# Weight conversions let go earlier, and key features computed from the PSUM bank with the row maximum as bias, in a linear-attention and mixer kernel

## The chip, the cores and the metric

The kernel runs on one core of one Trainium2 chip. The metric is the time of one execution on the device in microseconds. The kernel before took 1147.82 us in the median of 3 runs (1147.16 to 1151.01).

## The reference

Linear attention over 8 batches, 8 heads, 576 tokens and 64 values a head, and behind it a mixer block (token mixing, then channel mixing), all in float32:

```
proj = x @ w_phi                                   # 64 -> 128 features
proj = proj - max(|proj|)  per token
phi  = concat(exp(proj), exp(-proj))               # for q and for k
kv, z = sum over tokens of k_phi * v, of k_phi
attn = (q_phi @ kv) / (q_phi @ z + 1e-6)
h = relu(x^T @ w_tok1) @ w_tok2                    # mixes the 576 tokens
u = x + h^T
out = u + relu(u @ w_ch1) @ w_ch2                  # 512 -> 1536 -> 512
```

## The kernel before

**Work and streams.** Heads are taken in 32 pairs: pair `i` holds two heads of batch `i // 4`. Five generators emit the work: `keys()`, `queries()`, `token_stream()`, `load_weights()` and `channel_stream()`. `weave` (line 628) calls them by a virtual clock with a share for each, and the framework's scheduler then fixes the order in which each engine takes its instructions. An engine takes them strictly in that order, so an instruction that waits holds all behind it.

**Keys.** A pair has five groups of keys, four of two 128-token units and a last one of a single unit. For a group TensorE makes the projection `ppk` (line 242 for the plain float32 pairs 0 to 7), VectorE reduces it to the largest absolute value `mxk` (line 252) and subtracts it into an SBUF tile `pmk` (line 254), ScalarE makes the exponentials `kp` of plus and minus `pmk` (line 298), and TensorE adds their products with the values into `pkv` (line 323). Pairs 0 to 3 use two banks of PSUM by turns for `ppk`; from pair 4 on there is a single one, under the tag `keys`. A bank is free for the next projection when all its readers are done: here the reduction and the subtraction.

**Queries.** They go the same way (`ppq`, `mxq`, `pmq`), then are transposed (`pt`, line 392), exponentiated (`qf`, line 399) and multiplied with `kv` into `pr` (line 430). For each pair and each of the two token segments VectorE normalises: an add of 1e-6 to the denominators `dn` (line 443), a reciprocal (444) and a product into `rows` (445).

**Conversions.** The weights arrive as float64 bits. `convert` (line 127) loads them with a DMA on the SyncE (SP) queue into one of four staging buffers, takes the absolute value on ScalarE (line 146), makes the float32 bits with four VectorE operations (lines 147 to 150), rounds them to the upper half on ScalarE (line 74) and leaves the lower half to a subtraction on GpSimd (line 77). There are 24 conversions of 128x512 for the channel mixing (tiles `bitsc`, weights `wc`), in the order: four of the first matrix, four of the second, and so three times. Channel mixing (`h` and `acc`, line 83) cannot begin its parts before they are converted.

**Gates.** `row_numerators` appends the denominators of pairs 0 to 3 to the list `gates` (line 440): entry 2i is pair i's first segment, 2i+1 its second. Conversion n waits for entry `GATES[n]`: in the emission by `turn_of` (line 156), and on the chip by a copy of one column on GpSimd (line 145), on which its absolute value waits. Conversions beyond the list wait for the last entry in the emission and get no copy:

```
GATES = [2, 3, 4, 5, 6, 6, 7, 7]
...
        g = GATES[min(n, len(GATES) - 1)]
        yield from until(lambda: len(gates) > g)
        return gates[g] if n < len(GATES) else None
```

Of the kernel before, what the change touches and what calls it, by code (L numbers as in the profile page):

```python
# [12 lines left out]
AF = mybir.ActivationFunctionType  # L13
ALU = mybir.AluOpType
# [4 lines left out]
B, H, S, D = 8, 8, 576, 64  # L19
NP = H // 2  # L20
# [5 lines left out]
PLAIN = 8  # L26
ROWS = 8
BURST = 8
GATES = [2, 3, 4, 5, 6, 6, 7, 7]
BORROWED = 18  # L30
STAGES = 4
LAST = 15
# [12 lines left out]
def mixer_kernel(ctx, tc, qk, vm, vt, w_phi, w1, w2, wc1, wc2d, out):  # L45
    nc = tc.nc

    cst = ctx.enter_context(tc.tile_pool(name="cst", bufs=1))
    wk = ctx.enter_context(tc.tile_pool(name="wk", bufs=2))
# [106 lines left out]
    def turn_of():  # L156
# [3 lines left out]
        ngated[0] += 1  # L160
# [56 lines left out]
    def less_max(ts, units, name, base=None, early=False):

        n, kind = len(units), name[0]
        if early and base == D:
            ps = ps_a.tile([P, 2, 2, F], F32, tag=f"a{nplain['k'] % 2}", name=f"pp{name}")
            nplain["k"] += 1
        elif early and base == 0 and (nplain["q"] % 2 == 0 or nplain["q"] >= BORROWED):
            ps = ps_h.tile([P, 2, 2, F], F32, tag="h", name=f"pp{name}")
            nplain["q"] += 1
        elif early and base == 0:
            ps = ps_w.tile([P, 2, 2, F], F32, tag="keys", name=f"pp{name}", bufs=1)
            nplain["q"] += 1  # L230
        elif kind == "k":
            ps = ps_w.tile([P, 2, 2, F], F32, tag="keys", name=f"pp{name}", bufs=1)
        else:
            ps = ps_w.tile([P, 2, 2, F], F32, name=f"pp{name}", **REST)
        for i, u in enumerate(units):
            t, c = (ts[1], 512) if u is None else (ts[u[0]], P * u[1])
            if base is None:
                nc.tensor.matmul(ps[:, i].rearrange("p two f -> p (two f)"), t[:, c:c + P],  # L238
                                 wp2.rearrange("p two f -> p (two f)"), start=True, stop=True)
            else:  # L240
                rows = slice(D, P) if name == "k0_0" else slice(0, P)
                nc.tensor.matmul(ps[:, i, 0], t[rows, c:c + P], wz[rows, base // D], start=True, stop=True)  # L242
# [12 lines left out]
        return pm

    nplain = {"k": 0, "q": 0}
    raws, pairs, kvs, loaded = {}, {}, {}, set()
# [2 lines left out]
    def load(i):  # L261

        raw = wk.tile([P, 2 * S], F32, tag="raw", name=f"raw{i}", bufs=1)
        lo, hi = (D if i <= PLAIN else 0), (D if i == B * NP else P)
        nc.sync.dma_start(raw[lo:hi], qk[i, lo:hi])
        raws[i] = raw

    def load_plain(i):

        out = []  # L270
        for k, (c, n) in enumerate(((0, 512), (512, 640))):
            t = wk.tile([P, n], F32, tag=f"{'kq'[i % 2]}{k}", name=f"pair{i}{k}", bufs=1)
            nc.sync.dma_start(t[D:], qk[i, D:, c:c + n])
            out.append(t)
        for k, (c, n) in enumerate(((0, 512), (512, 640))):
            nc.sync.dma_start(out[k][:D], qk[i + 1, :D, c:c + n])
        pairs[i] = out

    def keys():
        groups = [[(0, 0), (0, 1)], [(0, 2), (0, 3)], [(1, 0), (1, 1)], [(1, 2), (1, 3)], [None]]  # L280
        todo = None
        for i in range(B * NP):
            yield from until(lambda: i < 2 or i - 2 in asked)
            if i < PLAIN:
                load_plain(i)
            else:
                load(i)
            v_sb, queue = vtiles[i % 2], nc.sync if i else nc.scalar
            queue.dma_start(v_sb[:, 0:4].rearrange("p u j d -> p (u j) d")[:, :, :D], vm[i])
            for j in range(2):  # L290
                queue.dma_start(v_sb[j * D:(j + 1) * D, 4, j, :D], vt[i, j])
            plain = D if i < PLAIN else None
            ts = pairs[i] if i < PLAIN else stack(raws[i], D, f"k{i}")
            for g, us in enumerate(groups):
                pm = less_max(ts, us, f"k{i}_{g}", plain, i < NP)
                kp = wk.tile([P, 2, 2, F], F32, tag="kp", name=f"kp{i}_{g}")
                for sg in range(2):
                    nc.scalar.activation(kp[:, :len(us), sg], pm[:, :len(us)], AF.Exp, scale=1.0 - 2.0 * sg)  # L298
                yield 0.22
                if todo:  # L300
                    add_kv(*todo)
                    yield 0.82
                todo = (i, g, us, kp, v_sb)
        add_kv(*todo)
        yield 0.82
# [322 lines left out]
    def weave(streams):  # L628
# [3 lines left out]
        while streams:  # L632
# [58 lines left out]
```

## Time and profile before

| | |
|---|---|
| median of 3 runs | 1147.82 us |
| profiled execution, its own time | 1147.9 us |
| its span, first to last instruction | 1146.1 us |
| TensorE (PE) busy | 1117.9 us, 98% |
| VectorE (DVE) busy | 796.0 us, 69% |
| GpSimd (POOL) busy | 521.3 us, 45% |
| ScalarE (ACT) busy | 486.3 us, 42% |
| granted TensorE clock, mean | 0.995 |

The first three are one time seen three ways: what a run is timed at, what the profiled one took, and what its instructions span. The shares are means over a kernel whose stages differ, so a stage has to be looked at by itself. The granted clock is a share of full speed; it takes two levels, 1.0 (2.4 GHz) and 0.5 (1.2 GHz), and a figure between is a mean over a stretch.

### The profile page before, as it was taken

What the parts mean: (1) busy time and instruction counts of PE and PEld (TensorE: products, weight loads), DVE (VectorE), ACT (ScalarE), POOL (GpSimd) and SP (SyncE); (2) the same over time, 40 slices, a digit from 0 to 9 for tenths busy, and PEclk for the clock granted to TensorE, in tenths of its full rate; (3) what the DMA queues carried; (4) which work ended last, traced back from release to release, by engine and by line L of the source; (5) the groups of instructions that cost most, each with busy time, mean ns of one, the idle gap of its engine ahead of it and who ended that gap; (6) DMA issues with size and microseconds to landing.
All of it is one profiled execution on the core that took longest, in us unless ns stands there. A gap on an engine that the chain in (4) does not pass through costs nothing.

```text
span 1146.1 us, 24296 instructions
## 1 busy us (share of the span) xinstructions
PE 1117.9 (98%) x9280; PEld 1098.4 (96%) x9280; DVE 796.0 (69%) x1751; ACT 486.3 (42%) x1397; POOL 521.3 (45%) x671
## 2 busy tenths in 40 slices
PE   8998899999999999999999999999999999999998
PEld 7997799989999999999999999999999999999998
DVE  7779873478687797887787685775777878663111
ACT  4666552344444544444544343443454454331110
POOL 2234433265455565565555462653655656430000
PEclk9999899999999999999999999999999999999999
DMA  7534511111011111111111110111111110000000
GB/s 205 141 93 149 194 30 40 32 36 46 4 48 41 42 32 49 33 29 34 40 32 50 32 50 2 50 33 28 32 42 32 51 32 12 19 1 19 20 19 19
DMA packets 66164, 54.39 MB, mean 47 GB/s; under 512 B 44992, under 2 KB 56768, under 8 KB 66048
## 3 DMA queue, kind: packets, MB, share of 16 engines
q1 hardware_dynamic: 64528, 52.41, 15.7%
q8 instruction: 74, 1.21, 0.5%
q10 hardware_dynamic: 1520, 0.43, 0.2%
q14 instruction: 42, 0.34, 0.1%
HBM read 43.38 MB, written 9.44 MB: 46 GB/s over the span
## 4 chain that ended last, share of the span: by engine, by line
PE 84%; DVE 8%; DMA 2%; ACT 2%; POOL 2%; issue 1%; SPq 0%; DVEq 0%; POOLq 0%; ACTq 0%
PE h L83 25%; PE acc L83 25%; PE pkv L323 9%; PE pn L83 6%; PE ph L83 3%; PE pa L83 3%; PE pt L392 3%; PE pr L430 2%; PE ppk L238 2%; PE ppq L238 2%; DMA raw<-in_w 1%; DVE qh L76 1%; PE px L504 1%; PE ppq L242 1%; DVE bitsc L149 1%
## 5 line engine op out<-in xcount | busy, mean ns | idle before, releaser
L83 PE MATMUL acc<-gh,wc 128*128 128x256 f32 x1728 | 343.1, 283 | 0.0
L83 PEld LDWEIGHTS acc<-gh,wc 128*128 128x128 f32 x1728 | 275.3, 188 | 0.1
L83 PE MATMUL h<-uh,wc_h 128*128 128x256 f32 x864 | 245.5, 284 | 1.5 <-DVE gl L571 1.5
L83 PE MATMUL h<-uh,wc_l 128*128 128x256 f32 x864 | 245.0, 284 | 0.0
L83 PE MATMUL h<-ul,wc_h 128*128 128x256 f32 x864 | 243.5, 282 | 0.0
L83 PE MATMUL acc<-gl,wc 128*128 128x256 f32 x864 | 242.0, 282 | 0.0
L298 ACT ACTIVATE kp<-pmk 128x256 f32<-128x256 f32 (+1 forms) x320 | 109.3, 389 | 162.2 <-POOL pmk L254 141.4
L83 PEld LDWEIGHTS h<-uh,wc_h 128*128 128x128 f32 x864 | 162.6, 188 | 2.2 <-issue 1.3
L323 PE MATMUL pkv<-v,kp 128*128 128x65 f32 (+2 forms) x1152 | 160.7, 271 | 2.9 <-ACT kp L298 2.1
L83 PEld LDWEIGHTS h<-ul,wc_h 128*128 128x128 f32 x864 | 162.8, 188 | 0.1
L83 PEld LDWEIGHTS acc<-gl,wc 128*128 128x128 f32 x864 | 162.6, 188 | 0.0
L83 PEld LDWEIGHTS h<-uh,wc_l 128*128 128x128 f32 x864 | 162.5, 188 | 0.1
L323 PEld LDWEIGHTS pkv<-v,kp 128*128 128x128 f32 x1152 | 149.6, 193 | 4.6 <-ACT kp L298 3.0
L571 DVE SCALAR_TENSOR_TENSOR gl<-h,gh 128x512 fp32r<-128x512 f32 x108 | 73.8, 683 | 107.6 <-ACT gh L570 104.2
L77 POOL TENSOR_TENSOR ql<-qf,qh 128x320 fp32r<-128x320 f32 (+1 forms) x96 | 88.0, 916 | 116.3 <-DVE qh L76 103.5
L399 ACT ACTIVATE qf<-pt 128x320 f32<-128x320 f32 (+1 forms) x256 | 91.7, 411 | 95.7 <-PE pt L392 79.1
L570 ACT ACTIVATE gh<-h 128x512 fp32r<-128x512 f32 x108 | 64.9, 601 | 124.2 <-PE h L83 123.0
L76 DVE CAST qh<-qf 128x320 fp32r<-128x320 f32 (+1 forms) x192 | 90.2, 483 | 37.3 <-ACT qf L399 32.2
L83 PE MATMUL pn<-qh,kv 128*128 128x320 f32 (+1 forms) x384 | 99.7, 298 | 0.2 <-DVE qh L76 0.2
L551 POOL TENSOR_TENSOR ul<-xt,uh 128x64 fp32r<-128x64 f32 (+3 forms) x120 | 60.0, 525 | 82.6 <-ACT uh L550 81.9
L479 DVE RECIPROCAL den<-den 128x320 f32<-128x320 f32 (+1 forms) x48 | 93.5, 1949 | 0.9
L213 POOL TENSOR_TENSOR stk<-raw,stk 64x512 fp32r<-64x512 f32 (+1 forms) x48 | 68.9, 1436 | 47.2 <-DVE stk L212 38.7
(122 smaller groups left out, 2274.8 us busy)
## 6 DMA issues: line engine op xcount, KB each, us to landing
raw<-in_qk SPq DMA_DIRECT2D x23, 576.0 KB, 3.8
rawc<-in_wc SPq DMA_DIRECT2D x24, 512.0 KB, 4.2
v<-in_vm SPq DMA_DIRECT2D x31, 256.0 KB, 3.4
out_x<-xt SPq DMA_DIRECT2D x12, 256.0 KB, 2.1
out_x<-xt SPq DMA_DIRECT2D x16, 192.0 KB, 2.0
pair<-in_qk SPq DMA_DIRECT2D x16, 160.0 KB, 4.1
pair<-in_qk SPq DMA_DIRECT2D x16, 128.0 KB, 3.7
raw<-in_w SPq DMA_DIRECT2D x8, 256.0 KB, 5.0
```

Source lines behind the costliest of these rows:

```text
L76: eng_hi.tensor_copy(hi, raw)
L77: eng_lo.tensor_tensor(lo, raw, hi.bitcast(F32), op=ALU.subtract)
L83: nc.tensor.matmul(o, a, m, start=first and i == 0, stop=last and i == 2, skip_group_check=group_ok)
L213: nc.gpsimd.tensor_tensor(t[lo:lo + D], src, t[base:base + D].bitcast(F32), op=ALU.subtract)
L238: nc.tensor.matmul(ps[:, i].rearrange("p two f -> p (two f)"), t[:, c:c + P], wp2.rearrange("p two f -> p (two f)"), start=True, stop=True)
L298: nc.scalar.activation(kp[:, :len(us), sg], pm[:, :len(us)], AF.Exp, scale=1.0 - 2.0 * sg)
L323: nc.tensor.matmul(o, kp[:, n, sg], v, start=g == 0 and n == 0 and sg == 0, stop=u is None, skip_group_check=True)
L399: nc.scalar.activation(full, src, AF.Exp, scale=1.0 - 2.0 * sg)
L479: nc.vector.reciprocal(den, den)
L551: nc.gpsimd.tensor_tensor(l[:, d:d + n], t[:, c, o:o + n], h[:, d:d + n].bitcast(F32), op=ALU.subtract)
L570: nc.scalar.activation(gh, ph, AF.Relu)
L571: nc.vector.scalar_tensor_tensor(gl, ph, 0.0, gh.bitcast(F32), op0=ALU.max, op1=ALU.subtract)
```

## The change

It has two parts. First, the list `GATES` is longer and starts lower: nine conversions instead of six are let go by entry 6 (the first segment of pair 3, the fourth pair) or before, the first one by entry 1 instead of 2, and twelve instead of eight get a gate copy. Second, for the keys of pairs 2 to 7 the subtraction falls away. VectorE only negates the maximum into a column `nmx` (one buffer for all groups), and ScalarE reads the projection from its bank, with the negated maximum as bias for the positive exponential and the maximum itself for the negative one. As the bias belongs to a unit, a group of two units takes four ACTIVATEs of 128 columns instead of two of 256. The bank is now released by the last of them.

```
--- before.py
+++ after.py
@@ -26,7 +26,7 @@
 PLAIN = 8
 ROWS = 8
 BURST = 8
-GATES = [2, 3, 4, 5, 6, 6, 7, 7]
+GATES = [1, 2, 2, 3, 4, 4, 5, 6, 6, 7, 7, 7]
 BORROWED = 18
 STAGES = 4
 LAST = 15
@@ -250,9 +250,13 @@
             pr, eng = ps[:, :n, 0], nc.vector
         mx = column(wk, 2, tag=f"mx{kind}", name=f"mx{name}")
         nc.vector.tensor_reduce(mx[:, :n], pr, axis=AX.X, op=ALU.max, apply_absolute_value=True)
+        if base == D and not name.startswith(("k0_", "k1_")):
+            nmx = column(wk, 2, tag="nmx", bufs=1, name=f"nmx{name}")
+            nc.vector.tensor_scalar(nmx[:, :n], mx[:, :n], -1.0, None, op0=ALU.mult)
+            return pr, (nmx, mx)
         pm = wk.tile([P, 2, F], F32, tag=f"pm{kind}", name=f"pm{name}", bufs=1 if kind == "t" else 2)
         eng.tensor_tensor(pm[:, :n], pr, mx[:, :n].unsqueeze(2).to_broadcast([P, n, F]), op=ALU.subtract)
-        return pm
+        return (pm, None) if kind == "k" else pm
 
     nplain = {"k": 0, "q": 0}
     raws, pairs, kvs, loaded = {}, {}, {}, set()
@@ -292,10 +296,15 @@
             plain = D if i < PLAIN else None
             ts = pairs[i] if i < PLAIN else stack(raws[i], D, f"k{i}")
             for g, us in enumerate(groups):
-                pm = less_max(ts, us, f"k{i}_{g}", plain, i < NP)
+                pm, mx = less_max(ts, us, f"k{i}_{g}", plain, i < NP)
                 kp = wk.tile([P, 2, 2, F], F32, tag="kp", name=f"kp{i}_{g}")
                 for sg in range(2):
-                    nc.scalar.activation(kp[:, :len(us), sg], pm[:, :len(us)], AF.Exp, scale=1.0 - 2.0 * sg)
+                    if mx is None:
+                        nc.scalar.activation(kp[:, :len(us), sg], pm[:, :len(us)], AF.Exp, scale=1.0 - 2.0 * sg)
+                        continue
+                    for u in range(len(us)):
+                        nc.scalar.activation(kp[:, u, sg], pm[:, u], AF.Exp, scale=1.0 - 2.0 * sg,
+                                             bias=mx[sg][:, u:u + 1])
                 yield 0.22
                 if todo:
                     add_kv(*todo)
```

The list of numbers moves instructions on every engine. In the rows below `bitsc_e_c` or `bitsc_k` is the tile of a conversion, and lines after 252 are higher by 4 or 9 in the changed file (`pmq` 258, denominators 452 to 454, `kp` 303 or 306).

VectorE, the first conversion. Before, it stands among the queries and keys behind the denominators of pair 1's first segment (`dn_0_549`):

```order
L443 TENSOR_SCALAR dn_0_549<-pr_0_506 128x4
L444 RECIPROCAL dn_0_549<-dn_0_549 128x4
L252 TENSOR_REDUCE mxq_00_635<-ppq_00_632 128x2
L445 TENSOR_TENSOR rows_0_361<-pr_0_506,dn_0_549 128x2x2x64
L443 TENSOR_SCALAR dn_0_549<-pr_0_506 64x2
L252 TENSOR_REDUCE mxq_01_701<-ppq_01_698 128x2
L254 TENSOR_TENSOR pmq_00_637<-ppq_00_632,mxq_00_635 128x256
L444 RECIPROCAL dn_0_549<-dn_0_549 64x2
L252 TENSOR_REDUCE mxk_1_723<-ppk_1_720 128x2
L147 TENSOR_SCALAR bitsc_0_0_558<-bitsc_0_0_558 128x512
```

Now it stands behind the denominators of pair 0's second segment (`dn_1_447`), ahead of pair 1's (`dn_0_564`):

```order
L452 TENSOR_SCALAR dn_1_447<-pr_1_404 128x4
L453 RECIPROCAL dn_1_447<-dn_1_447 128x4
L252 TENSOR_REDUCE mxt_658<-ppt_656 128x1
L454 TENSOR_TENSOR rows_0_361<-pr_1_404,dn_1_447 128x2x2x64
L252 TENSOR_REDUCE mxk_3_636<-ppk_3_633 128x2
L147 TENSOR_SCALAR bitsc_0_0_453<-bitsc_0_0_453 128x512
L148 TENSOR_SCALAR bitsc_0_0_453<-bitsc_0_0_453 128x512
L258 TENSOR_TENSOR pmt_660<-ppt_656,mxt_658 128x128
L149 SCALAR_TENSOR_TENSOR bitsc_0_0_453<-rawc_0_0_451,bitsc_0_0_453 128x512
L258 TENSOR_TENSOR pmq_11_621<-ppq_11_616,mxq_11_619 128x256
L150 SCALAR_TENSOR_TENSOR bitsc_0_0_453<-rawc_0_0_451,bitsc_0_0_453 128x512
L255 TENSOR_SCALAR nmxk_3_638<-mxk_3_636 128x2
L452 TENSOR_SCALAR dn_0_564<-pr_0_519 128x4
```

It moved up by one segment, and all its four operations now lie where the old order had keys and queries alone.

VectorE, the last key group of pair 5 (`ppk_4`). Before, its subtraction `pmk_4_1507` runs amid the conversions of the second third (`2_512`, `3_512`, and `4` of the second matrix):

```order
L252 TENSOR_REDUCE mxk_4_1505<-ppk_4_1503 128x1
L444 RECIPROCAL dn_0_1370<-dn_0_1370 64x2
L147 TENSOR_SCALAR bitsc_3_512_1335<-bitsc_3_512_1335 128x512
L148 TENSOR_SCALAR bitsc_2_512_1303<-bitsc_2_512_1303 128x512
L147 TENSOR_SCALAR bitsc_4_1384<-bitsc_4_1384 128x512
L254 TENSOR_TENSOR pmk_4_1507<-ppk_4_1503,mxk_4_1505 128x128
L445 TENSOR_TENSOR rows_0_1369<-pr_0_1259,dn_0_1370 64x128
L148 TENSOR_SCALAR bitsc_3_512_1335<-bitsc_3_512_1335 128x512
L149 SCALAR_TENSOR_TENSOR bitsc_2_512_1303<-rawc_2_512_1301,bitsc_2_512_1303 128x512
```

Now the negation `nmxk_4_1573` in its place stands amid those of the last third (`2_1024`, `3_1024`):

```order
L149 SCALAR_TENSOR_TENSOR bitsc_2_1024_1553<-rawc_2_1024_1551,bitsc_2_1024_1553 128x512
L148 TENSOR_SCALAR bitsc_3_1024_1597<-bitsc_3_1024_1597 128x512
L252 TENSOR_REDUCE mxq_01_1762<-ppq_01_1759 128x2
L252 TENSOR_REDUCE mxk_4_1571<-ppk_4_1569 128x1
L150 SCALAR_TENSOR_TENSOR bitsc_2_1024_1553<-rawc_2_1024_1551,bitsc_2_1024_1553 128x512
L149 SCALAR_TENSOR_TENSOR bitsc_3_1024_1597<-rawc_3_1024_1595,bitsc_3_1024_1597 128x512
L258 TENSOR_TENSOR pmq_01_1764<-ppq_01_1759,mxq_01_1762 128x256
L255 TENSOR_SCALAR nmxk_4_1573<-mxk_4_1571 128x1
L150 SCALAR_TENSOR_TENSOR bitsc_3_1024_1597<-rawc_3_1024_1595,bitsc_3_1024_1597 128x512
L252 TENSOR_REDUCE mxk_0_1651<-ppk_0_1648 128x2
L255 TENSOR_SCALAR nmxk_0_1653<-mxk_0_1651 128x2
```

Measured by conversions, the keys of pair 5 slid back: by that point ten conversions were finished before, and nineteen now.

ScalarE at the same place. Before, the group's exponentials come in one row (two ACTIVATEs, out of `pmk`), a row of pair 6 seven rows later:

```order
L146 ACTIVATE bitsc_4_1384<-rawc_4_1382 128x512
L146 ACTIVATE bitsc_5_1412<-rawc_5_1410 128x512
L298 ACTIVATE kp_4_1509<-pmk_4_1507 128x128 x2
L457 COPY xt_1_1449<-pf_0_1451 128x320
L399 ACTIVATE qf_110_1515<-pt_11_1512 128x256
L399 ACTIVATE qf_111_1517<-pt_11_1512 128x256
L74 CAST wc_h<-bitsc_2_512_1303 128x512
L332 COPY kv_5_1640<-pkv_1296 128x260
L74 CAST wc_h<-bitsc_3_512_1335 128x512
L298 ACTIVATE kp_0_1588<-pmk_0_1586 128x2x128 x2
```

Now they read the bank `ppk_4_1569` and stand between the roundings of the last third:

```order
L74 CAST wc_h<-bitsc_1_1024_1530 128x512
L466 COPY xt_1_1518<-pf_1_1766 128x256
L74 CAST wc_h<-bitsc_2_1024_1553 128x512
L306 ACTIVATE kp_4_1575<-ppk_4_1569,nmxk_4_1573 128x128
L306 ACTIVATE kp_4_1575<-ppk_4_1569,mxk_4_1571 128x128
L74 CAST wc_h<-bitsc_3_1024_1597 128x512
L341 COPY kv_5_1709<-pkv_1359 128x260
L306 ACTIVATE kp_0_1655<-ppk_0_1648,nmxk_0_1653 128x128 x2
L306 ACTIVATE kp_0_1655<-ppk_0_1648,mxk_0_1651 128x128 x2
```

The exponentials of pair 6's first group follow four rows behind them, and they are four ACTIVATEs.

## Rows read from the trace of the kernel before

**Rows 1.** The page: the span; busy time, share of the span and instructions of each engine; and the granted TensorE clock in tenths in 40 equal slices of the span.

```profile
span 1146.1 us, 24296 instructions
...
PE 1117.9 (98%) x9280; PEld 1098.4 (96%) x9280; DVE 796.0 (69%) x1751; ACT 486.3 (42%) x1397; POOL 521.3 (45%) x671
...
PEclk9999899999999999999999999999999999999999
```

**Rows 2.** Sums by stretch (us from the span's start): its length, then busy time and instructions of PE, of its weight loads, of DVE, ACT and POOL, then the granted clock, the DMA engines' busy share and GB/s.

```profile
35.00:78.40 43.40, 42.52 (x364) 40.75 (x362) 30.10 (x86) 25.02 (x70) 11.09 (x15) 1.00 0.47 129
78.40:133.30 54.90, 46.55 (x339) 43.04 (x338) 53.23 (x121) 33.84 (x80) 25.29 (x23) 0.91 0.47 149
...
146.00:240.00 94.00, 93.92 (x807) 92.69 (x807) 47.86 (x116) 35.69 (x99) 32.72 (x42) 1.00 0.10 31
```

**Rows 3.** Waits between 78.4 and 133.3 us: who waited for whom, us in total, how often, the longest.

```profile
ACT bitsc L146 <- DMA rawc<-in_wc: 4.6, 5, 1.4
...
PE ppk L242 <- DVE pmk L254: 2.6, 2, 2.4
...
PE ph L83 <- DVE xt L539: 1.7, 1, 1.7
PE pf L456 <- DVE rows L445: 1.6, 1, 1.6
...
PE ph L83 <- DVE al L530: 0.7, 1, 0.7
```

**Rows 4.** VectorE's instructions in order of time: start, duration, line, operation and tiles; in brackets the idle time before and what ended it. Three places of the same stretch.

```profile
78.45 0.16 DVE L443 TENSOR_SCALAR dn<-pr 128x4 f32<-128x4 f32 x1 [2.16 <-PE pr L430]
...
114.13 0.41 DVE L252 TENSOR_REDUCE mxq<-ppq 128x2 f32<-128x256 f32 x1
114.46 0.40 DVE L254 TENSOR_TENSOR pmk<-ppk,mxk 128x256 f32<-128x256 f32 x1
...
115.82 1.76 DVE L149 SCALAR_TENSOR_TENSOR bitsc<-rawc,bitsc 128x512 uint32<-128x512 uint32 x1
...
133.05 0.39 DVE L254 TENSOR_TENSOR pmk<-ppk,mxk 128x256 f32<-128x256 f32 x1
```

**Rows 5.** VectorE's instructions by line and form between 78.4 and 133.3 us: count, busy us in all, mean ns of one, and the engine's idle time before them.

```profile
L149 DVE SCALAR_TENSOR_TENSOR bitsc<-rawc,bitsc 128x512 uint32<-128x512 uint32 x14 | 13.0, 934 | 0.0
L150 DVE SCALAR_TENSOR_TENSOR bitsc<-rawc,bitsc 128x512 uint32<-128x512 uint32 x13 | 10.6, 825 | 0.0
L147 DVE TENSOR_SCALAR bitsc<-bitsc 128x512 f32<-128x512 f32 x14 | 8.7, 624 | 0.1
L148 DVE TENSOR_SCALAR bitsc<-bitsc 128x512 uint32<-128x512 uint32 x14 | 6.6, 476 | 0.0
L254 DVE TENSOR_TENSOR pmk<-ppk,mxk 128x256 f32<-128x256 f32 x9 | 3.7, 411 | 0.0
L252 DVE TENSOR_REDUCE mxk<-ppk 128x2 f32<-128x256 f32 x9 | 3.7, 410 | 0.1
...
L444 DVE RECIPROCAL dn<-dn 128x4 f32<-128x4 f32 x5 | 0.8, 169 | 0.0
...
L254 DVE TENSOR_TENSOR pmk<-ppk,mxk 128x128 f32<-128x128 f32 x2 | 0.6, 276 | 0.0
```

**Rows 6.** Sums by stretch as in rows 2, in slices of 2 us.

```profile
114.00:116.00 2.00, 1.08 (x5) 1.08 (x6) 2.00 (x6) 1.34 (x3) 2.00 (x2) 0.66 0.83 262
116.00:118.00 2.00, 1.85 (x9) 1.55 (x8) 2.00 (x3) 1.07 (x2) 1.03 (x1) 0.50 0.95 301
...
120.00:122.00 2.00, 1.14 (x7) 0.88 (x7) 2.00 (x5) 1.92 (x5) 1.23 (x1) 0.86 0.30 47
122.00:124.00 2.00, 2.00 (x10) 1.88 (x10) 2.00 (x6) 1.00 (x4) 0.04 (x1) 0.50 1.01 406
124.00:126.00 2.00, 2.00 (x11) 1.88 (x12) 2.00 (x6) 0.48 (x1) 0.00 (x0) 0.50 0.19 76
126.00:128.00 2.00, 2.00 (x10) 1.67 (x9) 1.84 (x5) 0.00 (x0) 0.00 (x0) 0.50 0.00 0
```

**Rows 7.** VectorE in order of time, the four operations of the fourth conversion, ahead of the stretch of rows 3 to 5.

```profile
72.45 0.42 DVE L147 TENSOR_SCALAR bitsc<-bitsc 128x512 f32<-128x512 f32 x1
72.90 0.43 DVE L148 TENSOR_SCALAR bitsc<-bitsc 128x512 uint32<-128x512 uint32 x1
73.36 0.69 DVE L149 SCALAR_TENSOR_TENSOR bitsc<-rawc,bitsc 128x512 uint32<-128x512 uint32 x1
74.08 0.70 DVE L150 SCALAR_TENSOR_TENSOR bitsc<-rawc,bitsc 128x512 uint32<-128x512 uint32 x1
```

**Rows 8.** ScalarE's exponentials by form between 78.4 and 133.3 us, as in rows 5; `pmk` lies in SBUF, `pt` in PSUM.

```profile
L298 ACT ACTIVATE kp<-pmk 128x256 f32<-128x256 f32 x16 | 5.8, 414 | 1.8 <-DVE pmk L254 1.7
...
L399 ACT ACTIVATE qf<-pt 128x256 f32<-128x256 f32 x10 | 3.3, 381 | 1.8 <-PE pr L430 1.3 <-PE pt L392 0.5
...
L298 ACT ACTIVATE kp<-pmk 128x128 f32<-128x128 f32 x4 | 1.0, 300 | 0.3 <-DVE pmk L254 0.3
```

**Rows 9.** GpSimd in order of time: two subtractions for lower halves in one row (x2), and a single one.

```profile
112.86 4.16 POOL L77 TENSOR_TENSOR wc_l<-bitsc,wc_h 128x512 fp32r<-128x512 f32 x2 [5.81 <-ACT wc_h L74]
118.21 1.28 POOL L77 TENSOR_TENSOR wc<-bitsc,wc 128x512 fp32r<-128x512 f32 x1 [1.18 <-ACT wc L74]
```

More of the change, by code (lines that the diff above doesn't have):

```diff
@@ L28 @@
 BURST = 8
-GATES = [2, 3, 4, 5, 6, 6, 7, 7]
+GATES = [1, 2, 2, 3, 4, 4, 5, 6, 6, 7, 7, 7]
 BORROWED = 18
@@ L252, in less_max @@
         nc.vector.tensor_reduce(mx[:, :n], pr, axis=AX.X, op=ALU.max, apply_absolute_value=True)
+        if base == D and not name.startswith(("k0_", "k1_")):
+            nmx = column(wk, 2, tag="nmx", bufs=1, name=f"nmx{name}")
+            nc.vector.tensor_scalar(nmx[:, :n], mx[:, :n], -1.0, None, op0=ALU.mult)
+            return pr, (nmx, mx)
         pm = wk.tile([P, 2, F], F32, tag=f"pm{kind}", name=f"pm{name}", bufs=1 if kind == "t" else 2)
         eng.tensor_tensor(pm[:, :n], pr, mx[:, :n].unsqueeze(2).to_broadcast([P, n, F]), op=ALU.subtract)
-        return pm
+        return (pm, None) if kind == "k" else pm
     nplain = {"k": 0, "q": 0}
@@ L294, in keys @@
             for g, us in enumerate(groups):
-                pm = less_max(ts, us, f"k{i}_{g}", plain, i < NP)
+                pm, mx = less_max(ts, us, f"k{i}_{g}", plain, i < NP)
                 kp = wk.tile([P, 2, 2, F], F32, tag="kp", name=f"kp{i}_{g}")
                 for sg in range(2):
-                    nc.scalar.activation(kp[:, :len(us), sg], pm[:, :len(us)], AF.Exp, scale=1.0 - 2.0 * sg)
+                    if mx is None:
+                        nc.scalar.activation(kp[:, :len(us), sg], pm[:, :len(us)], AF.Exp, scale=1.0 - 2.0 * sg)
+                        continue
+                    for u in range(len(us)):
+                        nc.scalar.activation(kp[:, u, sg], pm[:, u], AF.Exp, scale=1.0 - 2.0 * sg,
+                                             bias=mx[sg][:, u:u + 1])
                 yield 0.22
```

## The prediction

> **What bounds the kernel.** I read the page first, then sums by stretch, then the waits inside the one bad stretch. TensorE (PE) is busy 1117.9 us of a span of 1146.1 [rows 1]; the profiled execution took 1147.9 us, 1.8 more than its span and 0.1 over the median of 1147.82. So time can only come out of the places where PE stands still or runs at half clock. The sums show one such place [rows 2]: from 146 to 240 us PE works 93.92 of 94.00 us with 807 matmul records (a float32 matmul makes two), or 0.1164 us per record, the pace at full clock. From 78.4 to 133.3 us it gets through only 339 records in 54.9 us. At full pace they need 339 x 0.1164 = 39.5 us, so 15.4 us are lost there, and VectorE (DVE) is busy 53.23 of the 54.9. Before it, from 35 to 78.4, PE loses 0.9 us and DVE is busy 30.10 of 43.40: DVE has 13.3 us free.
>
> The waits of the bad stretch agree [rows 3]: PE's waits end with DVE work (pmk 2.6, xt 1.7, rows 1.6, al 0.7). So DVE's list between two places sets this stretch: from the add on the denominators of pair 4's first segment, which DVE begins at 78.45 after waiting 2.16 us for PE, to the pmk of pair 6's fourth group at 133.05 [rows 4].
>
> **The change: what DVE no longer does.** For pairs 2 to 7 the subtraction pmk goes (24 of 128x256, 6 of 128x128); a negation of 2 numbers comes in its place. Large DVE operations start 0.33 us apart (114.13, 114.46) while their mean is 0.41 [rows 4, 5], so I price the large ones 0.08 under their means. The negation has no row. From below it is free; above, the reciprocal of 128x4 at 0.169 [rows 5]. I take 0.10, a small operation that overlaps as the large ones do. Whole kernel: 24 x (0.33 - 0.10) + 6 x (0.20 - 0.10) = 6.1 us less on DVE. That is not the gain: only DVE's list up to the place where PE waits counts.
>
> **What moves.** In the new order seven conversions instead of four stand before the denominators of pair 4's first segment. That is three times 2.24 us (0.42 + 0.43 + 0.69 + 0.70) [rows 7], 6.7 us, less 13 subtractions swapped for negations, 11 x 0.23 + 2 x 0.10 = 2.7. The 4.0 us go into the 13.3 us that DVE has free from 35 to 78.4 [rows 2]: price 0. Without that cover the bounds are -0.9 (PE's whole loss there disappears) and +1.0 (a quarter of the extra work shows).
>
> But keys slid back against conversions. Before, the sharpest place is pair 6's fourth group. Now a crowd of conversions stands ahead of pair 5's **last** group: DVE negates that maximum only after 19 conversions and three of the four operations of the twentieth, while before ten were done when the pmk of that group ran (the order above). PE needs the exponentials of that group for its next pkv, and pair 6's first projection needs the bank that those free. So the new stretch ends there. Counted in the two orders from the same denominators to the end:
> - before: 121 DVE instructions, 54.9 us; PE 339 records.
> - after: 106 DVE instructions; PE 262 records, 262 x 0.1164 = 30.5 us.
>
> DVE's time after, from the difference of the two lists: one conversion less, 0.93 + 0.82 + 0.62 + 0.47 - 4 x 0.08 = 2.5; nine large pmk, 3.0; two small, 0.4; four mxk, 1.3; one mxq and one pmq, 0.7; one denominator add and reciprocal, 0.2; against them one xt more, 0.3, and seven negations, 0.7. Net 7.0 less [rows 5], 47.9 us if DVE's idle 1.7 us (54.9 - 53.23) comes back, 46.2 if not. I take 47.0. PE's loss is then 47.0 - 30.5 = 16.5 against 15.4: **+1.1 us** (+0.3 to +2.0). DVE does less, but it must be done 77 records earlier. Behind that place four conversions are left over many records, and PE loses only what it does now (0.08 us from 146 to 240).
>
> **The clock.** In the bad stretch the granted clock falls to 0.50, the lower level of 1.2 GHz, from 116 to 118 and again from 122 to 128, both behind slices with PE busy for little over half (1.08 and 1.14 of 2.00) [rows 6]. From 122 to 128 PE is busy all 6 us at half clock, and DVE is busy for 5.84 of them: what PE loses is hidden under DVE. After the change DVE has little left at that point and PE a full queue, so the same half-clock stretch would be paid. Bounds: 0, and half of the 6 us, 3.0. I take 1.0, a third, since part of it will fall into the waiting itself. The Trainium skill, page TensorE: Matmul & The Clock Gate, section HAM oscillation, says that a burst of matmuls behind idle gaps starts throttled, and that each gap is paid again; by that rule this term would be the full 3.0. By that rule the second drop is no accident, and the trace agrees: it stands behind the slice with 1.14 of 2.00 busy.
>
> **Queues.** ScalarE takes each group of keys as four ACTIVATEs of 128 columns with a column as bias, in place of two of 256. The nearest rows are 0.30 for 128 columns from SBUF, 0.41 for 256, and 0.38 for 256 out of a bank [rows 8]; four at 0.22 to 0.30 are 0.9 to 1.2 us against 0.7 to 0.8. Seven groups in the stretch add 0.5 to 3.5 us to an engine that is idle for over a third of it (33.84 of 54.9) [rows 2]: price 0, unless a release waits for it (third rival). The Trainium skill, page ScalarE: Activation LUTs, section What ACT_TABLE_LOAD costs, speaks against the change here: it gives 93 ns more for each ACTIVATE with a pointer operand; by it an estimate is 0.4 us more per group, and the sum would stay, as ScalarE is still not full. No run here has shown such a bias yet. GpSimd gets four more gate copies in an engine busy 25.29 of 54.9: 0. On SP the conversions' loads now stand ahead of more pair loads, and behind a load that waits for its staging buffer the pair loads wait too; ScalarE's waits for such loads were 4.6 us in all [rows 3] under DVE's shadow, so 0, at most +1. The negated column has one buffer: DVE must wait for the two exponentials of the group before. In the order other DVE and ScalarE work lies between; 0, at most +1.
>
> **Sum:** 1147.9 + 1.1 + 1.0 = **1150.0 us**, 0.19% over the median: no change, leaning slow. Own range of this case: from the lower bounds of all terms, 1147.9 + 0.3 - 0.9 = 1147.3, to the upper ones of the stretch and the clock, 1147.9 + 2.0 + 3.0 = 1152.9.
>
> **Rivals.**
> - *Faster: less crowding* (0.28). A conversion costs DVE 2.84 us in the bad stretch and 2.24 just before it [rows 5, 7]; one L149 took 1.76 at 115.82 while two GpSimd subtractions took 4.16 instead of 2 x 1.28 [rows 4, 9]. If starting earlier spaces DVE's and GpSimd's halves apart, 13 conversions give back up to 13 x 0.6 = 7.8: 1147.9 + 1.1 - 7.8 = 1141.2; half of it 1145.1. It decides when the mean L149 of the stretch is under 0.75 (0.934 now). Against it: the conversions stand even closer.
> - *Slower: the clock after the burst* (0.23). Place: the first 6 to 7 us behind pair 5's last group. PE has fewer matmuls between DVE's releases than now and then a full queue at half clock. Price 3.0, and 1.7 more if the first drop is also paid (2 us at 0.50, and 0.66 for 2 us, which is 1.4 us at 0.50): 1147.9 + 1.1 + 4.7 = 1153.7. It decides as soon as PE is busy over 90% at 0.50 while DVE is idle. For it: rows 6; against it: the waits may end at another phase.
> - *Slower: the single bank* (0.07). From pair 4 on all key projections share one bank, which DVE freed with pmk and ScalarE now frees with its fourth exponential, some 0.6 us later (4 x 0.22 to 0.30 against one pmk of 0.33 to 0.41). Seven groups in the stretch: 7 x 0.6 = 4.2, at 1147.9 + 1.1 + 4.2 = 1153.2. It decides when that release, not the negation, comes last. For it: PE already waited 2.6 us for pmk [rows 3].
> - That the change does not do what it says is ruled out by the order: 30 pmk are gone, and the first conversion stands a segment earlier.
>
> **Numbers.** The forecast has 0.42. About 0.3% (3.4 us) is what a measurement of this kernel can tell from no change: under 1144.4 is faster, over 1151.3 slower. Of the first rival 0.23 lies under 1144.4 and 0.05 above (less than half the relief). Of the forecast 0.36 lies between and 0.06 over 1151.3, where the clock is paid in full. Of the clock rival 0.20 is slower and 0.03 between; the bank's 0.07 is slower. So faster 0.23, same 0.36 + 0.05 + 0.03 = 0.44, slower 0.06 + 0.20 + 0.07 = 0.33. The range leaves out the far end of the fast case and the tail of the slow ones, two in ten: 1142.0 to 1155.5.
>
> **What would show it.** Right: DVE full from about 78 to about 125; a long wait of PE that ends with kp (line 306) of pair 5's last group, near 124 to 127; a stretch of clock 0.50 behind it; from 150 on PE full again; DVE's total about 6 us lower and all conversions done ahead of pair 7's first key group. Wrong if PE makes its records in the bad stretch faster than one per 0.15 us (55 / 339 = 0.162 now, 47 / 262 = 0.179 forecast), if the mean L149 falls under 0.75, or if PE's waits name kp in pairs 4 and 5 one group after another (the single bank).

## The result, and the profile after

The changed kernel takes 1154.73 us (median of 5 runs, 1153.10 to 1155.16) against 1147.51 beside it: ratio 1.0052, 95% interval 1.0037 to 1.0066 (the two medians alone would give 1.0063). So it is slower, by a little more than the 0.3% that the prediction took as the least that can be told from no change. The profiled execution took 1153.33 us, 5.4 more than that of before, and so did its span (1151.5 against 1146.1).

The page of the changed kernel: span, busy time by engine, and the granted clock in 40 slices.

```profile
span 1151.5 us, 24387 instructions
PE 1119.5 (97%) x9280; PEld 1100.7 (96%) x9280; DVE 788.5 (68%) x1751; ACT 495.3 (43%) x1445; POOL 525.4 (46%) x675
PEclk9999799999999999999999999999999999999999
```

VectorE (DVE) does 7.5 us less (796.0 before), and TensorE (PE) still sets the time. So I count PE's matmul records by stretch, as for before. Sums by stretch of the kernel before (the columns are those of [rows 2]):

```profile
0.00:78.40 78.40, 74.08 (x588) 69.24 (x588) 56.18 (x166) 43.10 (x118) 19.25 (x37) 1.00 0.58 158
78.40:140.00 61.60, 52.96 (x392) 49.23 (x391) 59.77 (x135) 37.69 (x90) 29.27 (x26) 0.92 0.48 153
140.00:400.00 260.00, 255.66 (x2141) 251.23 (x2141) 175.16 (x393) 111.62 (x328) 125.25 (x159) 1.00 0.13 37
```

The same stretches of the changed kernel, and the two parts of the bad one:

```profile
0.00:78.40 78.40, 74.13 (x579) 68.51 (x580) 62.34 (x177) 51.01 (x145) 24.23 (x43) 1.00 0.67 176
78.40:140.00 61.60, 47.30 (x337) 44.18 (x337) 54.10 (x123) 34.93 (x88) 31.56 (x25) 0.86 0.45 139
140.00:400.00 260.00, 257.45 (x2165) 253.88 (x2164) 164.64 (x390) 113.67 (x341) 121.17 (x155) 1.00 0.12 35
...
78.70:128.93 50.23, 35.93 (x263) 33.54 (x263) 45.55 (x107) 29.74 (x76) 28.46 (x23) 0.89 0.44 132
...
128.93:140.00 11.07, 11.07 (x71) 10.41 (x72) 8.54 (x17) 5.13 (x13) 3.10 (x3) 0.73 0.48 161
```

At 0.1164 us per record: by 78.4 us PE is 9 records behind (1.0 us), from 78.4 to 140 another 55 (6.4 us), and from 140 to 400 it wins back 24 (2.8 us). That leaves 4.7 of the 5.4 us.

What PE waits for between 30 and 150 us in the changed kernel (us in total, times, longest):

```profile
PE pkv L332 <- ACT kp L306: 11.2, 4, 4.3
PE pa L83 <- POOL xl L77: 2.5, 2, 2.2
PE pf L465 <- DVE rows L454: 1.3, 1, 1.3
...
PE ppk L242 <- ACT kp L306: 0.2, 1, 0.2
```

The waits of [rows 3] (pmk, xt, rows, al) are gone but for the rows. In their place PE waits for exponentials of keys (`kp`), and for GpSimd. The two longest are those of pair 5's fourth and last groups. In order of time, PE's first matmuls behind them, in the changed kernel:

```profile
120.61 1.73 PE L332 MATMUL pkv<-v,kp 128*128 128x128 f32 x6 [4.28 <-ACT kp L306]
...
128.93 1.23 PE L332 MATMUL pkv<-v,kp 128*128 128x130 f32 x4 [3.70 <-ACT kp L306]
```

What VectorE did between the maximum of each of those groups (mxk) and its negation (nmxk):

```profile
115.23 0.41 DVE L252 TENSOR_REDUCE mxk<-ppk 128x2 f32<-128x256 f32 x1
115.56 0.27 DVE L252 TENSOR_REDUCE mxt<-ppt 128x1 f32<-128x128 f32 x1
117.16 0.78 DVE L147 TENSOR_SCALAR bitsc<-bitsc 128x512 f32<-128x512 f32 x1 [1.33 <-ACT bitsc L146]
117.86 1.78 DVE L150 SCALAR_TENSOR_TENSOR bitsc<-rawc,bitsc 128x512 uint32<-128x512 uint32 x1
119.56 0.41 DVE L252 TENSOR_REDUCE mxq<-ppq 128x2 f32<-128x256 f32 x1
119.90 0.15 DVE L255 TENSOR_SCALAR nmxk<-mxk 128x2 f32<-128x2 f32 x1
...
125.86 0.28 DVE L252 TENSOR_REDUCE mxk<-ppk 128x1 f32<-128x128 f32 x1
126.06 1.41 DVE L150 SCALAR_TENSOR_TENSOR bitsc<-rawc,bitsc 128x512 uint32<-128x512 uint32 x1
127.40 0.68 DVE L149 SCALAR_TENSOR_TENSOR bitsc<-rawc,bitsc 128x512 uint32<-128x512 uint32 x1
128.00 0.41 DVE L258 TENSOR_TENSOR pmq<-ppq,mxq 128x256 f32<-128x256 f32 x1
128.33 0.14 DVE L255 TENSOR_SCALAR nmxk<-mxk 128x1 f32<-128x1 f32 x1
```

Conversions stand between the maximum and the 0.15 us that PE needs. In the first case there is an idle 1.33 us as well, for ScalarE, which itself waited 2.1 us for GpSimd's subtractions (`wc`).

Behind the second wait the clock is at its lower level. Sums by 2 us of the changed kernel:

```profile
130.00:132.00 2.00, 2.00 (x10) 1.72 (x10) 0.86 (x3) 0.89 (x2) 1.25 (x1) 0.50 1.04 350
132.00:134.00 2.00, 2.00 (x12) 2.00 (x11) 0.61 (x3) 1.85 (x6) 0.03 (x1) 0.50 0.48 172
```

From 130 to 134 PE is full at 0.50 (1.2 GHz) while VectorE has 1.47 us of work in 4: the half clock that VectorE's list hid before [rows 6] is now paid.

### The profile page after: what moved, and what is told of

The parts are those of the page before. It is cut to its first block, busy times and chain, and to the rows that moved or that the text cites. A ratio compares the mean times of both kernels' runs of the same rounds, so it can differ in the third digit from the quotient of the medians.

```text
span 1151.5 us, 24387 instructions
## 1 busy us (share of the span) xinstructions
PE 1119.5 (97%) x9280; PEld 1100.7 (96%) x9280; DVE 788.5 (68%) x1751; ACT 495.3 (43%) x1445; POOL 525.4 (46%) x675
## 4 chain that ended last, share of the span: by engine, by line
PE 84%; DVE 9%; POOL 2%; issue 2%; ACT 2%; DMA 1%; SPq 0%; DVEq 0%; POOLq 0%; ACTq 0%
PE h L83 25%; PE acc L83 25%; PE pkv L332 9%; PE pn L83 6%; PE ph L83 3%; PE pa L83 3%; PE pt L401 3%; PE ppk L238 2%; PE ppq L238 2%; PE pr L439 2%; DVE qh L76 1%; PE px L513 1%; PE ppk L242 1%; PE ppq L242 1%; DVE bitsc L150 1%
## 5 line engine op out<-in xcount | busy, mean ns | idle before, releaser
L332 PE MATMUL pkv<-v,kp 128*128 128x65 f32 (+2 forms) x1152 | 164.7, 271 | 12.9 <-ACT kp L306 11.2
L303 ACT ACTIVATE kp<-pmk 128x256 f32<-128x256 f32 x260 | 88.8, 389 | 140.1 <-POOL pmk L258 134.6
```

Source lines behind the costliest of these rows:

```text
L332: nc.tensor.matmul(o, kp[:, n, sg], v, start=g == 0 and n == 0 and sg == 0, stop=u is None, skip_group_check=True)
```

## The experiments

All twelve change the changed kernel, or the kernel before, in one or two places. The theories: **A**, the crowd: VectorE's conversions stand too close together ahead of PE's needs. **B**, the key path: negation and four exponentials make every group slower. **C**, the earlier gates cost by themselves. **N**, it is VectorE's negation. **D**, conversions that come too late hold up the first channel block.

The table gives what each order has and what it took. "Ahead" counts the conversions that VectorE has finished, in its order, ahead of the subtraction or negation of pair 5's last key group and of pair 6's fourth (where ScalarE negates, of the maximum). The next columns are PE's records and mean granted clock from 78.4 to 140 us and its records from 140 to 400 us. The last ones are the median and the ratio to the kernel before, run beside it: its median was 1147.51 us beside the change, 1149.30 beside e1 to e4, 1148.19 beside e5 to e8 and 1149.24 beside e9 to e12, so kernels run beside different ones are best compared by the ratio. The records are those of the one profiled execution, which can lie 2 us or more from the median (e2 1147.51, e6 1147.53, e4 1147.29).

| kernel | ahead | 78.4–140 | 140–400 | us | ratio (95%) |
|---|---|---|---|---|---|
| before | 10 / 17 | 392, 0.92 | 2141 | 1147.51 | |
| the change | 19 / 22 | 337, 0.86 | 2165 | 1154.73 | 1.0052 (1.0037–1.0066) |
| e1 gates | 12 / 18 | 421, 0.94 | 2164 | 1142.08 | 0.9942 (0.9929–0.9955) |
| e2 keys | 15 / 19 | 382, 0.92 | 2164 | 1149.55 | 1.0008 (0.9997–1.0018) |
| e3 change, ScalarE negates | 17 / 22 | 420, 0.92 | 2165 | 1144.80 | 0.9969 (0.9957–0.9982) |
| e4 change, share 6 | 17 / 20 | 417, 0.92 | 2143 | 1145.34 | 0.9973 (0.9959–0.9988) |
| e5 keys, ScalarE negates | 15 / 19 | 394, 0.89 | 2141 | 1147.09 | 0.9993 (0.9984–1.0002) |
| e6 change, share 4 | 14 / 17 | 488, 1.00 | 2066 | 1150.10 | 1.0017 (1.0003–1.0031) |
| e7 change, ScalarE negates, share 6 | 16 / 19 | 478, 1.00 | 2142 | 1140.31 | 0.9937 (0.9924–0.9949) |
| e8 gates, share 6 | 12 / 17 | 481, 1.00 | 2155 | 1134.09 | 0.9885 (0.9871–0.9898) |
| e9 old keys, crowd | 16 / 21 | 341, 0.92 | 2133 | 1155.14 | 1.0056 (1.0041–1.0072) |
| e10 before, share 6 | 10 / 14 | 476, 1.00 | 2074 | 1147.01 | 0.9990 (0.9979–1.0001) |
| e11 gates, share 5 | 12 / 16 | 499, 1.00 | 2099 | 1143.11 | 0.9954 (0.9938–0.9970) |
| e12 keys, share 6 | 14 / 17 | 473, 1.00 | 2068 | 1149.82 | 1.0008 (0.9996–1.0020) |

**e1 and e2: each half alone.**

```
e1 (from before)   -GATES = [2, 3, 4, 5, 6, 6, 7, 7]
                   +GATES = [1, 2, 2, 3, 4, 4, 5, 6, 6, 7, 7, 7]
e2 (the change)    -GATES = [1, 2, 2, 3, 4, 4, 5, 6, 6, 7, 7, 7]
                   +GATES = [2, 3, 4, 5, 6, 6, 7, 7]
```

> Only the list of gates is changed; keys stay as in the kernel before. In its order VectorE has done 12 conversions ahead of pair 5's last key group (10 before the change, 19 with the whole change) and 18 ahead of pair 6's fourth (17 before). Theory A, the crowd: what the change costs is the number of conversions that VectorE must do ahead of pair 5's last key group, some 2.8 us each, and the half clock behind PE's wait there. Then this kernel's sharpest place is still pair 6's fourth group, with 14 conversions from pair 4's first group to it against 15 before, and it takes 1144 to 1148.5 us. Theory B, the key path: the negation and the four exponentials with a bias make each key group slower, wherever the conversions stand. Then nothing is lost here: 1147.5 us. Theory C, the gates alone: earlier conversions steal VectorE from the early part and the stretch: 1152 us or more.

> Only the keys of pairs 2 to 7 are changed; the gates stay as in the kernel before. 15 conversions stand ahead of pair 5's last key group. Theory A, the crowd: between the two kernels, nearer to the one before, since pair 6's fourth group (19 conversions, two more than before, 5.6 us, against some 13 subtractions less, 4.3 us) stays the sharpest place: 1147 to 1150.5 us. Theory B, the key path: the whole loss comes with this half: 1153 to 1156 us. Theory C, the gates alone: 1145 to 1148 us.

The gates alone are 0.58% faster, and the keys alone make no difference. So C falls, and B does as the cause of the whole loss. A gave 1144 to 1148.5 us for e1, so it too was short of what the gates win. The loss is neither half's: by themselves they would add up to about 0.5% faster, and together they are 0.5% slower. What they share is the order: 12 and 15 conversions ahead of pair 5's last group become 19.

**e3 and e4: the whole change with one thing less.**

```
e3  -nc.vector.tensor_scalar(nmx[:, :n], mx[:, :n], -1.0, None, op0=ALU.mult)
    +nc.scalar.mul(nmx[:, :n], mx[:, :n], -1.0)
e4  -(load_weights(), 10.0, False)
    +(load_weights(), 6.0, False)
```

> The whole change, but the negated maximum is made by ScalarE (one operation of 2 columns) and not by VectorE. VectorE's list loses 30 negations; 17 conversions instead of 19 stand ahead of pair 5's last key group, 14 instead of 17 ahead of its fourth. Theory A, the crowd: 2 x 2.8 us of VectorE less and six negations of 0.2 us less ahead of that place: 1147 to 1150.5 us. Theory B, the key path: if it is the lateness of the negation in VectorE's list (maximum at 115.23, negation at 119.90 us), the same, 1147 to 1151; if it is ScalarE's four exponentials, one more operation on ScalarE for each group makes it 1154.5 to 1157 us.

> The whole change, but the stream of conversions gets a share of 6.0 instead of 10.0 in the weaving, so they are spread further. The order is the same up to pair 5's third group; 17 conversions instead of 19 stand ahead of pair 5's last key group and 20 instead of 22 ahead of pair 6's fourth. Keys are made as in the changed kernel. Theory A, the crowd: 2 x 2.8 us less ahead of pair 5's last group: 1148 to 1151.5 us. Theory B, the key path: nothing of it is changed: 1153.5 to 1155.5 us.

Both take back more than the loss, and e4 doesn't touch how keys are made. B is out. Both lie below A's bands: two conversions less are 5.6 us, and each gave more than 9. Where the rest went was not separated. e3 leaves open how much is the negation, since its order has changed too.

**e5: the negation alone.** e2 with e3's edit.

> Only the keys of pairs 2 to 7 (the gates of the kernel before), with the negated maximum made by ScalarE. As with VectorE's negation (1149.55 us), 15 conversions stand ahead of pair 5's last key group and 19 ahead of pair 6's fourth, so the two differ in the negation alone. Theory A, the crowd (the count of conversions ahead of pair 5's last key group decides): 1147.5 to 1150 us. Theory N, the negation on VectorE decides (it takes 0.60 us in the stretch of that run and stands late in the list): 1141 to 1145.5 us.

With the order of conversions the same but for one or two places (pair 5: 6, 10, 11, 13, 15 here; 6, 9, 10, 13, 15 in e2), the ratio is 0.0015 lower, with intervals that overlap: the negation on VectorE costs at most a few us. N falls as the main cause. (1147.09 us lies 0.4 us under A's band and 1.6 over N's.)

**e6 and e7: how far the crowd can be spread.** e6 is the change with `(load_weights(), 4.0, False)`, e7 is e3 and e4 together.

> The whole change with VectorE's negation, and a share of 4.0 instead of 10.0 for the stream of conversions. 14 conversions stand ahead of pair 5's last key group (19 with the whole change, 17 at a share of 6.0, which took 1145.34 us), 17 ahead of pair 6's fourth, and the last of them behind pair 7. Theory A, the crowd: another three conversions, up to 8.4 us of VectorE, leave the place ahead of pair 5's last group: 1138 to 1143 us. Theory N, the negation: as at a share of 6.0, 1144 to 1147 us. Theory D: the late conversions now hold up the first channel block, and 1147 us or more come out.

> The whole change, with ScalarE's negation and a share of 6.0 together; apart they took 1144.8 and 1145.34 us against 1154.73. 16 conversions stand ahead of pair 5's last key group and 19 ahead of pair 6's fourth. Theory A: both are the same remedy for the same place, and what is left is small: 1140 to 1144 us. Theory N, with the crowd as a second cause of its own: the two gains add up, 1134 to 1138 us. Theory D: as with the share of 6.0 alone, 1144 to 1147 us, since the late conversions bind.

e6 comes out as D said: the bad stretch is gone (488 records, clock 1.00 throughout), and from 140 to 400 PE makes 2066 records instead of 2165, so 99 x 0.1164 = 11.5 us are given back. Where, by stretch, first the changed kernel and then e6:

```profile
160.00:180.00 20.00, 20.00 (x172) 19.43 (x172) 6.43 (x19) 7.11 (x23) 1.27 (x1) 1.00 0.01 2
240.00:260.00 20.00, 18.44 (x150) 17.77 (x148) 14.16 (x30) 9.19 (x28) 12.04 (x17) 1.00 0.14 38
...
160.00:180.00 20.00, 17.74 (x141) 16.96 (x142) 18.33 (x33) 12.09 (x34) 12.80 (x14) 1.00 0.23 70
240.00:260.00 20.00, 15.83 (x109) 14.36 (x108) 15.08 (x31) 8.25 (x25) 8.52 (x13) 0.91 0.21 59
```

31 of the 99 are lost from 160 to 180 us, where e6 still converts and VectorE is busy for 18.33 of 20 us. Another 41 are lost from 240 to 260 us, where no conversion is left. So the mechanism of D, conversions that hold up the first channel block, is borne out for a third; what makes the later place worse was not tried. e7 is A as forecast.

**e8 and e11: the gates with a share.** Old keys, e1's gates, and a share of 6.0 or 5.0.

> Only the gates are changed (that alone took 1142.08 us), and the stream of conversions has a share of 6.0. The order of conversions against keys is the same up to pair 6's second group; 17 instead of 18 stand ahead of pair 6's fourth, 20 instead of 24 ahead of pair 7's last. Theory A: one conversion less ahead of the sharpest place: 1139 to 1141.8 us. Theory D: the conversions left behind hold up the first channel block: 1143 us or more.

> The gates alone with a share of 5.0 (6.0 took 1134.09 us). 16 conversions instead of 17 ahead of pair 6's fourth key group and 20 as there ahead of pair 7's last. Theory A: little is left to win in the stretch: 1132 to 1135 us. Theory D: conversions that come later hold up the first channel block: 1135.5 us or more.

e8 beats both kernels, the one before by 1.15%, and does better than any theory said (1139 to 1141.8 us was A's): with one conversion less ahead of pair 6's fourth group than e1 PE makes 60 records more in the stretch, and one conversion at 2.8 us would be 24. The bad stretch in e8:

```profile
78.40:140.00 61.60, 58.39 (x481) 55.46 (x481) 54.06 (x131) 37.01 (x93) 24.40 (x26) 1.00 0.49 145
```

What is different is that the clock never falls: 1.00 against 0.94 in e1. e11 goes one step too far, as D said: 18 records more in the stretch, 56 fewer behind it.

**e9: the loss without the new keys.** Kernel before with

```
-GATES = [2, 3, 4, 5, 6, 6, 7, 7]
+GATES = [1, 2, 2, 3, 4, 4, 5, 5, 5, 6, 6, 6, 6, 6, 6, 6]
-(load_weights(), 10.0, False)
+(load_weights(), 14.0, False)
```

> Keys as in the kernel before (subtraction by VectorE); 16 gates (1, 2, 2, 3, 4, 4, 5, 5, 5, 6 seven times) and a share of 14.0 for the conversions, chosen so that the crowd is moved ahead without the new keys: 4 conversions ahead of pair 4's first key group, 16 ahead of pair 5's last (12 with the gates alone, which took 1142.08 us) and 21 ahead of pair 6's fourth (18 there). Theory A, the crowd: three to four conversions more in the stretch than with the gates alone, 8.4 to 11.2 us of VectorE: 1148 to 1154 us. Theory B, the key path (the new keys cost by themselves): there are none here, 1141 to 1144 us.

Theory A, just above its band: with the old keys the loss is as large as that of the change (1.0056 against 1.0052), and so are the records of the stretch (341, 337). PE's waits in it, 30 to 150 us:

```profile
PE ppk L242 <- DVE pmk L254: 3.3, 5, 0.9
PE pt L392 <- DVE pmq L254: 2.5, 2, 1.8
PE pf L456 <- DVE dn L443: 1.9, 1, 1.9
PE pf L456 <- DVE rows L445: 1.6, 3, 1.0
```

The crowd doesn't even need the same place: here it is spread over short waits for VectorE, none over 2 us. Nor do the two lose alike: from 78.4 to 140 us VectorE is idle for 7.5 of 61.6 us in the changed kernel, and for 3.4 in e9 (58.21 busy).

**e10 and e12: a share of 6.0 with the old gates.** e10 is the kernel before with it, e12 is e2 with it.

> The kernel before with a share of 6.0 for the conversions, nothing else. 14 conversions instead of 17 stand ahead of pair 6's fourth key group, 17 instead of 23 ahead of pair 7's last. Theory A: three conversions, 8.4 us, leave the sharpest place, and with the shorter waits the half clock goes too: 1136 to 1142 us. Theory D: without earlier gates the late conversions hold up the first channel block: 1144 us or more.

> Only the keys are changed (gates of the kernel before, VectorE's negation), with a share of 6.0. 14 conversions ahead of pair 5's last key group (15 at a share of 10.0, 1149.55 us) and 17 ahead of pair 6's fourth (19). Theory A: it loses only what its crowd costs, one to two conversions less than at a share of 10.0: 1142 to 1147 us. Theory B: the new keys cost 11 us wherever the conversions stand, as between the gates at a share of 6.0 without (1134.09) and with them (1145.34): 11 us over the kernel before at a share of 6.0, which runs beside this one.

e10 comes out as D said: 476 records in the stretch, but 2074 behind it. That may be what the earlier gates are good for: in e8 20 conversions are done ahead of pair 7's last key group, in e10 17. e12 fits neither theory. It is 2.8 us over e10 where B said 11 and A 1142 to 1147 us. The bad stretch is as good as e10's (473), so the new keys cost nothing there; 15 records are lost ahead of it (578 by 78.4 us against 593), 8 of them in the first 20 us, before any negation, and 6 behind it.

Part of that early loss goes with VectorE's negation. The first one stands near 30 us in every order that has one, so I count PE's records from 20 to 78.4 us. With the new gates they are 468, 464 and 469 where VectorE negates (the change, e4, e6), 481 and 481 where ScalarE does (e3, e7), and 481, 490 and 482 with old keys (e1, e8, e9). VectorE's negation goes with 12 to 17 records less than ScalarE's, 1.4 to 2.0 us. With the old gates they are 471 and 475 (e2, e12), 481 (e5), and 476 and 481 with old keys (before, e10).

Taken together, A is right in its direction and not in its price. Its bands held in e2 and e7; e1, e3, e4, e5 and e8 were faster, e9 slower, and e6, e10 and e11 took what D gave. The counts do not put the kernels in order either: with 16 and 21 conversions ahead e9 makes 341 records in the stretch, with 17 and 20 e4 makes 417, with 17 and 22 e3 makes 420. So it is shown that moving conversions makes the loss (e9) and takes it away (e4), and not what one conversion costs.

## Why the prediction was right or wrong

1. **The place** was right. The stretch ends with the exponentials of pair 5's last group (128.93 us; 124 to 127 was said), with 263 records in it (262 counted). From 150 to 240 us PE is full, and all conversions stand ahead of pair 7's keys.
2. **VectorE's work in it** came out a little under the sum: 45.55 us busy, where 46.2 had been worked out. **The stretch term failed**: it took 50.23 us and not 47.0 (46.2 to 47.9), because VectorE stood idle for 50.23 - 45.55 = 4.7 us, where 0 to 1.7 had been taken. PE lost 50.23 - 263 x 0.1164 = 19.6 us against 15.4: +4.2, forecast +1.1, upper bound +2.0.
3. **The step behind it is the one on queues**, which I priced at nothing. Two of VectorE's waits, 2.02 and 1.33 us, 3.35 of the 4.7, end with ScalarE, which stood behind GpSimd. The first, on VectorE:

```profile
82.10 1.28 DVE L149 SCALAR_TENSOR_TENSOR bitsc<-rawc,bitsc 128x512 uint32<-128x512 uint32 x2
83.31 1.28 DVE L150 SCALAR_TENSOR_TENSOR bitsc<-rawc,bitsc 128x512 uint32<-128x512 uint32 x2
86.61 0.42 DVE L518 TENSOR_TENSOR xs<-rows,xs 64x256 fp32r<-64x256 f32 x1 [2.02 <-ACT xs L517]
```

and on GpSimd, the subtractions xl that ScalarE and PE waited for, and two more of the same form later:

```profile
80.96 4.90 POOL L77 TENSOR_TENSOR xl<-rows,xh 128x256 fp32r<-128x256 f32 x2 [1.53 <-ACT xh L74]
...
91.12 1.82 POOL L77 TENSOR_TENSOR xl<-rows,xh 128x256 fp32r<-128x256 f32 x2 [0.86 <-ACT xh L74]
```

While VectorE ran the slow operations of two conversions without a gap (82.10 to 84.59), GpSimd's pair took 4.90 us; the later pair, with none of them beside it, took 1.82. [Rows 9] has a row like it; I used it for a rival that gains, and not for what a second conversion beside the first would do to the queue. It is not so each time: in the kernel before, three subtractions of this form with one slow operation beside them (at 56.23, 81.94 and 91.04 us) took 0.72 to 0.92 us each. That VectorE stretches GpSimd is read from such rows, and that the queue makes the loss from this one trace: no run changes the queue alone.

4. **The clock** was undersized. From 128.93 to 140 us PE needs 11.07 us for 71 records, 11.07 - 71 x 0.1164 = 2.8 lost, where I took a third of 3.0. Before lost 0.5 from 133.3 to 140, so the difference is 2.3. The Trainium skill (TensorE: Matmul & The Clock Gate, HAM oscillation) says that a burst behind idle gaps starts throttled; by it I had said 3.0, and the trace agrees with 2.8. No run separates half clock from crowd: the six kernels whose clock stays at 1.00 in the stretch make 473 to 499 records there, the eight others 337 to 421.
5. **The early part** was at its upper bound, 1.0 us. The largest gap is between 50 and 55 us (31 records against 38; other slices go both ways). There PE waits 0.97 us at 52.78 for the exponentials of a group whose negation took 1.04 us, and then needs 1.23 us for six matmuls that take 0.83 where no exponential is late (95.37). Before, it waited there too, 0.68 us for ScalarE, so not all of the gap is the negation's.
6. **The negation** was mis-sized for the whole kernel, and not for the stretch. I took 0.10 us each, 0.169 at most. The seven from 78.7 to 128.93 us took 0.139 to 0.169; the long ones lie elsewhere, up to 1.04 at 51.28, so they bear on the early part and not on the stretch term. Measured, by form in the whole run of the changed kernel, with the exponentials that replace those of [rows 8]:

```profile
L255 DVE TENSOR_SCALAR nmxk<-mxk 128x2 f32<-128x2 f32 x24 | 7.8, 326 | 0.7
...
L306 ACT ACTIVATE kp<-ppk,mxk 128x128 f32<-128x128 f32 x54 | 17.3, 373 | 0.0
L306 ACT ACTIVATE kp<-ppk,nmxk 128x128 f32<-128x128 f32 x54 | 17.2, 364 | 21.3 <-DVE nmxk L255 13.2 <-DVE dn L452 4.4 <-PE pf L465 1.8
```

Over the whole run a negation of 128x2 takes 0.326 us, where a subtraction took 0.41 ([rows 5]), so the swap gives back less than the 0.23 that I took; VectorE's total fell by 7.5 us all the same, where I had said about 6. The exponential with a column as bias takes 0.37 us against 0.30 for the same form without. The Trainium skill (ScalarE: Activation LUTs, What ACT_TABLE_LOAD costs) gives 93 ns for a pointer operand; 61 to 70 are seen here (303 ns for the form without), with a bank as source in place of SBUF, so the two are not cleanly compared. The price of a group held: four follow each other 0.26 us apart, some 1.1 us.

7. **Not foreseen**: the 2.8 us that come back from 140 to 400 us. e1, e2, e3 and e8 have them too (2155 to 2165 records), e4, e5, e7 and e9 not (2133 to 2143). 17 of the 24 records lie between 240 and 260 us (150, before 133). The cause was not tried.

Measured terms: +1.0 early, +4.2, +2.3 and -2.8 are 4.7 us; the forecast was +2.1. The time lies in the range, but "no change" was not the case that came, and that it lies there is partly luck: without the 2.8 us that I did not foresee it would be about 1157.5, over the end of the range at 1155.5. Of the **rivals**, the clock after the burst came nearest (1153.7), and its condition was met (PE 2.00 of 2.00 at 0.50, VectorE 0.86 and 0.61). Of the single bank nothing is seen: PE waits 0.2 us for that release. Less crowding shows how a sign can deceive: L149's mean did fall under the 0.75 named, and nothing was relieved.

VectorE's conversions by line in the changed kernel, 78.4 to 133.3 us:

```profile
L150 DVE SCALAR_TENSOR_TENSOR bitsc<-rawc,bitsc 128x512 uint32<-128x512 uint32 x13 | 12.8, 992 | 0.0
L149 DVE SCALAR_TENSOR_TENSOR bitsc<-rawc,bitsc 128x512 uint32<-128x512 uint32 x13 | 9.6, 744 | 0.0
```

L149 fell from 934 to 744 ns and L150 rose from 825 [rows 5] to 992: the slow one of the four operations has changed, and a conversion takes 2.82 us (2.86 before). The sum of the four was the gauge to name.

## What to carry to other kernels

Where a scheduler places filler work by what an engine has free, relief for that engine isn't kept as slack: it moves the filler forward, ahead of something that TensorE needs (with the keys alone, e2, 15 conversions stand ahead of pair 5's last group instead of 10). So read, in the new order, how much filler stands ahead of each operation that the binding engine waits for, and change density and start of the filler together: earlier gates alone gave 0.6%, a smaller share alone nothing, both 1.15%. The count is a warning and not a price, and the best share was found by running: at 5.0 in place of 6.0 the gain falls from 1.15% to 0.46%. And half clock that is hidden behind another engine can come to be paid when that engine gets done earlier, as from 130 to 134 us here.

## What the runs showed of the hardware

The negation of two numbers gets longer when GpSimd works beside it; the subtraction that it replaced does not. Up to 200 us of the changed kernel, the 12 negations of 128x2 beside which GpSimd's large subtractions in SBUF ran took 493 ns on average and up to 1044, the 12 others 160. In e2 it was 828 (7) against 164 (17). The negations of a single number (128x1, the last group of a pair) show none of it: in these two kernels the six beside such a subtraction took 139 to 156 ns, the six others 139 to 155. In the kernel before the subtraction out of a PSUM bank took 411 ns beside GpSimd's work (13) and 418 without (19). One case in e2, VectorE:

```profile
98.30 1.15 DVE L255 TENSOR_SCALAR nmxk<-mxk 128x2 f32<-128x2 f32 x1
106.45 0.15 DVE L255 TENSOR_SCALAR nmxk<-mxk 128x2 f32<-128x2 f32 x1
```

and GpSimd at the first of them:

```profile
96.28 3.14 POOL L77 TENSOR_TENSOR wc<-bitsc,wc 128x512 fp32r<-128x512 f32 x2
```

The long negation ends with GpSimd's second subtraction (99.45 and 99.42). Made by ScalarE, the same negation took 191 to 258 ns (e3).
